# Storing dk of head 58 in pieces of 9, 112 and 7 rows, and dq and o in two parts each

## The chip, the cores and the metric

One core of one Trainium2 chip. Times are device microseconds (us) of a whole execution; lower is better. In the traces 16 DMA engines serve the core.

## The reference, cut to what matters

```python
def _fwd_reference(q, k, v):                       # q: 2 x 32 x 1 x 128, k and v: 2 x 32 x 8192 x 128, bf16
    scale = q.shape[-1] ** -0.5
    scores = jnp.einsum("bhqd,bhkd->bhqk", q, k) * scale
    p = _softmax(scores, axis=-1)
    return jnp.einsum("bhqk,bhkd->bhqd", p, v)

def reference(q, k, v, grad_out):                  # [cut: wrapping]
    _out, _vjp = jax.vjp(_f, q, k, v)
    return (_out, *_vjp(grad_out))                 # o, dq, dk, dv
```

There are 64 heads (2 x 32) with one query row each. k and v of a head are 2 MB each, and dk and dv are as large. So the work is 128 loads and 128 stores of 2 MB, 537 MB in all, around little arithmetic.

## The kernel before

A tile holds k or v of one head: 128 rows (partitions) of 64 x 128 values, 16384 bytes a row. Twelve such tiles circulate. dk and dv are written into the same tile that k and v came in; it can be loaded again only when its store has landed.

```python
    def by_rows(eng, dst, src, rows):
        p = 0
        for m in rows:                             # one DMA for each piece of m rows
            pin(eng.dma_start(out=dst[p : p + m], in_=src[p : p + m], max_dma_last_dim=NT * D))
            p += m
```

The stores go out from GpSimd's queue (`store_eng`, q0 in the profile), the loads from SyncE's (`load_eng`, q1). dv and dk of the last head, in four pieces each, go out from SyncE too. Eight heads have dk split into 126 + 2 rows; all the others, head 58 among them, go as one DMA of 128 rows:

```python
SPREAD = range(4, 60, 7)                           # heads 4, 11, ... 53
# [cut]
            if w == 0 and i in SPREAD:
                by_rows(store_eng, dst, h.tile[w], (P - 2, 2))
            else:
                eng = load_eng if len(ends) > 1 else store_eng
                pin(eng.dma_start(out=dst[:, b0:b1, :], in_=h.tile[w][:, b0:b1, :]))
```

At the very start six rows of q are loaded from GpSimd after its engine cursor has been reset (`FIRST = 6`), which by the rule that the prediction quotes below leaves the cursor at 6. At the end dq and o, 64 rows of 256 bytes each, go out in one DMA each:

```python
    for w, (src, dst) in enumerate(((dqT, out_1), (oT, out_0))):
        # [cut: transpose on TensorE and copy into nat]
        load_eng.dma_start(out=dst.rearrange("b h s d -> (b h s) d"), in_=nat[:BH, 0, :])
```

## Time and profile before

| | before |
|---|---|
| median of the first three runs | 1282.16 us (1280.69 to 1282.3) |
| span of the profiled run, clock | 1284.2 us, 0.941 |
| data moved | 539 MB, 420 GB/s on average |
| last compute | about 1262 us |
| last landing | 1282.8 us |

The lines that say what bounds this kernel stand in the prediction below. The timeline of GpSimd before, from 1160 us on; its columns are start, length, engine, line, operation, what is written from what, and in brackets the idle time ahead of it and what ended that:

```profile
1167.96 0.53 POOL L445 DMA_DIRECT2D out_dram<-kvt  x1 [14.62 <-DVE kvt L427]
1176.11 0.53 POOL L445 DMA_DIRECT2D out_dram<-kvt  x1 [7.62 <-DVE qb L187]
1186.32 0.53 POOL L445 DMA_DIRECT2D out_dram<-kvt  x1 [9.68 <-DVE kvt L427]
1194.47 0.53 POOL L445 DMA_DIRECT2D out_dram<-kvt  x1 [7.63 <-DVE qb L187]
1205.72 0.53 POOL L445 DMA_DIRECT2D out_dram<-kvt  x1 [10.72 <-DVE kvt L427]
1213.88 0.53 POOL L445 DMA_DIRECT2D out_dram<-kvt  x1 [7.62 <-DVE qb L187]
```

The first line is dk of head 58, the next five are dv and dk of 59, dv and dk of 60, and dv of 61. Each is issued once VectorE has made its values (`DVE`). None waits for an earlier store here.

### The profile page before, as it was taken

Reading aid. Unit: us, or ns where it says so; the run is one execution under the profiler, and the core shown is the slowest. Engines: PE = TensorE matmul, PEld = TensorE weight load, DVE = VectorE, ACT = ScalarE, POOL = GpSimd, SP = SyncE. Lnnn points to the kernel's source line nnn. Section 1 sums busy time; section 2 is a strip of 40 time slices with the busy share of each in tenths; the row PEclk is TensorE's granted clock in tenths of the full one; section 3 lists DMA queues with packets and bytes.
Section 4 is the critical chain, followed back from the end, with each engine's and each line's share of the span. In section 5 each row is a group of like instructions: output and inputs, shape, how many; then the busy total and the mean of one; then the engine's idle time right before and its main releaser. Section 6 shows DMA issues by size and latency. Waiting matters only on the chain.

```text
span 1284.2 us, 32475 instructions
## 1 busy us (share of the span) xinstructions
PE 1099.4 (86%) x14148; PEld 805.5 (63%) x14148; DVE 1014.6 (79%) x2258; ACT 956.9 (75%) x641; POOL 76.0 (6%) x143
## 2 busy tenths in 40 slices
PE   6899899899889899889899889888888799879870
PEld 5666666666666666666666666666656566656650
DVE  2888888888888888888888888888788688777882
ACT  6777777778778778778778778777778687777750
POOL 0000000000000000000000000000000000000000
PEclk9999999999999999999999999999999899999985
DMA  9999999999999999999999999999999999999995
GB/s 388 427 428 428 428 429 428 427 428 428 428 428 428 420 428 428 428 424 426 428 428 418 425 428 428 422 418 426 428 427 419 422 429 429 426 423 429 428 413 219
DMA packets 40155, 539.03 MB, mean 420 GB/s; under 512 B 5196, under 2 KB 5196, under 8 KB 6476
## 3 DMA queue, kind: packets, MB, share of 16 engines
q1 hardware_dynamic: 20172, 272.70, 49.9%
q0 software_dynamic: 19840, 264.25, 48.8%
q8 instruction: 110, 1.80, 0.5%
q14 instruction: 33, 0.27, 0.1%
HBM read 268.47 MB, written 268.47 MB: 418 GB/s over the span
## 4 chain that ended last, share of the span: by engine, by line
DVE 32%; DMA 17%; issue 14%; another core or an unknown queue 14%; PE 12%; ACT 8%; POOL 1%; SPq 0%; ACTq 0%; POOLq 0%; DVEq 0%
DVE kvt L427 18%; DMA kvt<-in_v_dram 11%; ACT ev L196 8%; PE tp L194 7%; DMA out_dram<-kvt 6%; DVE sel L395 4%; DVE rows L221 3%; DVE sel L389 1%; PE acc L372 1%; DVE pair L303 1%; PE raw L208 1%; ACT E_f L271 1%; DVE dSu L349 1%; PE sw L178 1%
## 5 line engine op out<-in xcount | busy, mean ns | idle before, releaser
L196 ACT COPY ev<-tp 128x2048 bf16<-128x2048 bf16 x512 | 941.3, 1868 | 285.7 <-PE tp L194 280.6
L427 DVE TENSOR_TENSOR kvt<-qb,pair 128x2048 bf16<-128x2048 bf16 x512 | 616.9, 1216 | 0.1
L194 PEld LDWEIGHTS <-kvt 128*128 128x128 bf16 x8192 | 507.0, 102 | 160.7 <-issue 114.4
L194 PE MATMUL tp<-ident_bf,kvt 128*128 128x128 bf16 x8192 | 572.9, 226 | 38.0 <-DMA kvt<-in_v_dram 28.8
L208 PE MATMUL raw<-ev,qdT 128*32 128x512 bf16 x2048 | 210.0, 399 | 5.0 <-ACT ev L196 1.6
L395 DVE SCALAR_TENSOR_TENSOR sel<-acc,diag,sel 128x128 f32<-128x128 f32 x384 | 134.7, 351 | 13.6
L228 PEld LDWEIGHTS sw<-sel,rows 128*128 128x128 f32 x1024 | 124.8, 192 | 29.7 <-issue 12.9
L228 PE MATMUL sw<-sel,rows 128*128 128x16 f32 x1024 | 137.2, 266 | 0.6 <-DVE rl L324 0.6
L372 PE MATMUL acc<-kvt,E_pad 128*32 128x512 bf16 x1024 | 102.9, 391 | 30.6 <-DVE E_pad L280 30.6
L445 POOL DMA_DIRECT2D out_dram<-kvt x118 | 63.3, 536 | 1081.9 <-DVE kvt L427 518.1
L372 PE MATMUL acc<-kvt,dS_pad 128*32 128x512 bf16 x1024 | 111.1, 426 | 0.8 <-DVE dS_pad L358 0.8
L221 DVE COPY rows<-raw 128x512 f32<-128x512 f32 x128 | 87.5, 684 | 26.1 <-PE raw L208 26.1
L178 PE MATMUL sw<-ident_bf,qdT 128*128 128x128 bf16 x128 | 28.5, 223 | 70.9 <-DVE mp L240 70.8
L280 DVE CAST E_pad<-E_f 128x64 bf16<-128x64 f32 x64 | 12.5, 195 | 92.9 <-ACT E_f L271 92.9
L208 PEld LDWEIGHTS <-qdT 128*32 128x32 bf16 x2048 | 64.6, 95 | 25.0 <-issue 18.4
L315 PEld LDWEIGHTS sw<-ld,ones 128*128 128x128 f32 x256 | 38.2, 188 | 54.5 <-issue 29.3
L372 PEld LDWEIGHTS <-E_pad 128*32 128x32 bf16 x1024 | 26.3, 93 | 55.2 <-DVE E_pad L280 40.1
L246 DVE TENSOR_REDUCE gm<-sw 1x1 f32<-1x128 f32 x64 | 17.9, 279 | 49.3 <-PE sw L244 49.3
L409 PE MATMUL acc<-ones,sel 128*128 128x1 f32 x256 | 47.5, 255 | 6.2 <-DVE sel L395 6.2
L315 PE MATMUL sw<-ld,ones 128*128 128x1 f32 x256 | 49.1, 261 | 0.1
L409 PEld LDWEIGHTS acc<-ones,sel 128*128 128x128 f32 x256 | 44.0, 215 | 7.3 <-DVE sel L395 7.3
L389 DVE TENSOR_SCALAR sel<-acc,diag 128x128 f32<-128x128 f32 x128 | 43.8, 342 | 0.0
(49 smaller groups left out, 367.5 us busy)
## 6 DMA issues: line engine op xcount, KB each, us to landing
out_dram<-kvt POOLq DMA_DIRECT2D x118, 2048.0 KB, 51.5
kvt<-in_v_dram SPq DMA_DIRECT2D x64, 2048.0 KB, 19.1
kvt<-in_k_dram SPq DMA_DIRECT2D x63, 2048.0 KB, 19.4
out_dram<-kvt POOLq DMA_DIRECT2D x8, 2016.0 KB, 55.7
out_dram<-kvt SPq DMA_DIRECT2D x8, 512.0 KB, 23.2
kvt<-in_k_dram SPq DMA_DIRECT2D x2, 512.0 KB, 4.5
kvt<-in_k_dram SPq DMA_DIRECT2D x1, 1024.0 KB, 7.2
out_dram<-kvt POOLq DMA_DIRECT2D x8, 32.0 KB, 55.2
```

The lines of the kernel that those rows point to most:

```text
L194: pin(nc.tensor.transpose(tp[:, t, :], src[:, c * CH + t, :], ident_bf[:]))
L196: pin(nc.scalar.copy(out=ev[:], in_=tp[:]))
L208: nc.tensor.matmul(h.raw[g * SW : (g + 1) * SW, :], lhsT=qdT[:, w, q0 : q0 + SW], rhs=ev[:, g * QT : (g + 1) * QT, :].rearrange("p n d -> ...
L221: pin(nc.vector.tensor_copy(out=h.rows[:], in_=h.raw[:]))
L228: nc.tensor.matmul(h.score[w].rearrange("p (n t) -> p n t", t=QT)[:, :, t], lhsT=h.rows[:, t * P : (t + 1) * P], rhs=sel4[:].rearrange("p ...
L315: nc.tensor.matmul(out, lhsT=ones[:].to_broadcast([P, P]), rhs=col, start=True, stop=True)
L372: nc.tensor.matmul(h.acc[w][g : g + CW, :], lhsT=wts[:, n0 : n0 + CW], rhs=rows[:, n0 : n0 + QT, :].rearrange("p n d -> p (n d)"), start=( ...
L389: nc.vector.tensor_scalar(out=h.sel[:], in0=block, scalar1=diag[:, 0:1], scalar2=None, op0=ALU.mult)
L395: nc.vector.scalar_tensor_tensor(out=h.sel[:], in0=block, scalar=diag[:, b : b + 1], in1=h.sel[:], op0=ALU.mult, op1=ALU.add,)
L409: nc.tensor.matmul(h.acc[w][:, 0:1], lhsT=h.sel[:], rhs=ones[:], start=True, stop=True)
L427: nc.vector.tensor_tensor(out=h.tile[w][:, n0 : n0 + CH, :].rearrange("p n (e t) -> p n e t", t=2), in0=h.qb[w][:] .rearrange("p (e t) -> ...
L445: pin(eng.dma_start(out=dst[:, b0:b1, :], in_=h.tile[w][:, b0:b1, :]))
```

## The change

The intent, from its title: dk of head 58 is stored as 9, 112 and 7 rows so that two DMA engines (13 and 14) carry fewer rows near the end, and dq and o go out in two parts each. The title's "sums in four column groups" has no line in the diff; both kernels have that.

```diff
+LATE = 58
...
-            if w == 0 and i in SPREAD:
+            if w == 0 and i == LATE:
+                by_rows(store_eng, dst, h.tile[w], (9, P - 16, 7))
+            elif w == 0 and i in SPREAD:
                 by_rows(store_eng, dst, h.tile[w], (P - 2, 2))
...
-        load_eng.dma_start(out=dst.rearrange("b h s d -> (b h s) d"), in_=nat[:BH, 0, :])
+        rows = dst.rearrange("b h s d -> (b h s) d")
+        p = 0
+        for m in (44, 20) if w == 0 else (42, 22):
+            load_eng.dma_start(out=rows[p : p + m], in_=nat[p : p + m, 0, :], max_dma_last_dim=D)
+            p += m
```

## The prediction

> **What bounds the kernel now**
>
> I read the page from the top: the slices and queue totals first, then the queue's own waits, then the stretches, then the transfers of the last 20 us alone.
>
> ```profile
> PE 1099.4 (86%) x14148; PEld 805.5 (63%) x14148; DVE 1014.6 (79%) x2258; ACT 956.9 (75%) x641; POOL 76.0 (6%) x143
> ...
> DMA  9999999999999999999999999999999999999995
> GB/s 388 427 428 428 428 429 428 427 428 428 428 428 428 420 428 428 428 424 426 428 428 418 425 428 428 422 418 426 428 427 419 422 429 429 426 423 429 428 413 219
> ...
> q1 hardware_dynamic: 20172, 272.70, 49.9%
> q0 software_dynamic: 19840, 264.25, 48.8%
> ```
>
> No compute engine is full. The 16 DMA engines are, in every slice but the last: loads (q1) and stores (q0) take 98.7% of them at 428 GB/s. The time is data over DMA rate, plus two ends.
>
> ```profile
> SPq L100 <- DMA out_dram<-kvt: 1138.7, 116, 25.0
> ```
>
> The load queue spends 1138.7 us waiting for earlier stores to land: a tile is loaded again once its store is complete on all 16 engines, so the slowest engine paces the rest.
>
> ```profile
> 1180.00:1245.00 65.00, 53.53 (x725) 38.77 (x722) 51.85 (x114) 48.93 (x34) 3.19 (x7) 1.00 0.99 422
> 1245.00:1262.00 17.00, 7.89 (x42) 4.54 (x42) 15.49 (x35) 0.00 (x0) 0.53 (x1) 0.51 0.97 408
> 1262.00:1284.00 22.00, 0.00 (x0) 0.00 (x0) 0.01 (x1) 0.00 (x0) 0.00 (x0) 0.50 0.33 136
> ```
>
> Stretches: length, busy time of PE, weight loads, DVE, ACT, POOL, then clock, DMA share, GB/s. Compute ends at 1262; the last 22 us are DMA alone, one third busy. Which third, the same stretch in slices of 0.5 us from 1264 shows:
>
> ```profile
> GB/s 328 205 322 256 180 266 195 213 238 180 221 221 213 180 238 190 194 165 119 115 78 25 66 57 12 33 25 25 25 25 25 33 25 25 25 25 4 0 0 16
> ```
>
> One engine moves 16384 B in 0.6075 us (from one packet's start to the next's in the packet records), 27 GB/s. So half the engines are done by 1268, and the row of 25s, 1276.5 to 1282.1, is ONE engine finishing alone. The 16 landings of the last transfer (o) say it per engine: eight by 1267.9; six at 1272.7 to 1274.7; one at 1276.70; one at 1282.79, after which only 1.4 us of closing waits come. That one engine lags in all late stores: dk of head 58 lands there at 1233.6, on the next at 1222.7. Its landings come 9.72 us apart, 16 rows of 0.6075: it never idles. The end is therefore that engine's total of work, and a row taken off it is 0.61 us.
>
> **What the Trainium skill says**
>
> "DMA: Bandwidth & Descriptors", section "Why a DMA increments its semaphore by 16 and not by 1": a transfer runs on the largest k up to 16 that divides its rows; from GpSimd, on k consecutive engines from a cursor. The trace agrees for the 126 + 2 stores: stringing packets together (each starts 3 to 4 ns before the end of the one before on its engine) gives 14 engines with 18 packets of 8192 B and two with 2. For 112 rows the rule says k = 16, seven rows each, and nothing would be uneven. The change's title says otherwise; see the first rival.
>
> Same page, "Queues, rings and completion order": each engine takes turns between its queues, packet by packet. The trace agrees: the 9.72 us hold 8 store rows and 8 load rows.
>
> Same page, "Latency and other measured facts": engines 7 and 15 are usually slower. The records have no engine numbers, but one strung chain has 1251 packets some 30 ns too long. It is one of the two that the 126 + 2 splits relieve, and is not late at the end. The laggard is another engine: it has full-speed packets, plus the instruction packets of 16 KB (110 in all, about 0.95 us each) that only eight chains carry, 13 or 14 each.
>
> **The change part by part**
>
> 1. dk of head 58. Before, eight packets of 16384 B on every engine: 8 x 0.6075 = 4.86 us. After, in packets of 8192 B (0.3055 us). Nine rows leave the cursor nine further on. If the 112 run on 14 engines, eight rows each, and seven rows follow, then with the cursor at 6 (set by the six q rows, unmoved by a pair 14 + 2) the pieces cover 6 to 14; 15 to 12; 13 to 3. Engines 13 and 14 get one row from the first and one from the last: two rows, exactly the title. They need 4 x 0.3055 = 1.22 us, about 0.1 us more for the 4-byte packets that a left-out engine got in the earlier splits, so they save 3.5 us. The engines with nine rows pay 18 x 0.3055 - 4.86 = +0.64 us.
>
> 2. dq and o. 64 rows on 16 engines, four each, become 44 + 20 and 42 + 22: by the rule 11, 10, 14 and 11 engines, the lowest ones. Rows of 256 B take 0.014 us: an engine that loses all eight saves 0.11 us. Two more issues on SP at 0.5 us, hidden behind 20 us of DMA.
>
> 3. Side effect on POOL. The order of instructions shows each store waiting for the one eight issues before it; two more issues shorten that reach. The 7-row piece waits for dk of 55 (landed 1174.4, ready at 1168). dv of 59 waits for dv of 56 (1184.2 instead of 1176.1), then dk 59 1193.9 for 1186.3, dv 60 1203.6 for 1194.5, dk 60 1213.4 for 1205.7, dv 61 1224.5 for 1213.9: 8 to 11 us late. No load waits for these stores (the last load, issued at 1213.5, needs head 57), and the laggard has over 20 us of stores queued, so it never sees it. The five fast engines (dk 58 landed from 1183.5 on) lose some us and have 15 to spare. Cost on the path: 0.
>
> 4. Side effect on SP. The parts of o wait for the third and fourth piece of the last dv: landed 1270.3 and 1276.2 before. The fourth is the laggard's, so 1272.6 if it is relieved; with 1.5 us to the first landing (1265.6 to 1267.1 before), 1274. Hidden by 5 us.
>
> Sum: the laggard, if relieved, lands at 1282.79 - 3.5 - 0.1 = 1279.2. The next engine becomes 1276.70 + 0.64 = 1277.3 at worst, so the whole saving shows: -3.6 us, 0.28%. From the median: 1282.16 - 3.6 = 1278.6 us.
>
> **The rivals**
>
> A. The 112 rows run on 16 engines. Then every engine has 1 + 7 = 8 rows, the split does nothing and the end stays: 1282.1. For it: the rule as the page states it. Against: a title that names 13 and 14 fits only the 14-engine count, and the choice of 9 and 7 would be pointless.
>
> B. The relief misses the laggard. The trace does not number engines. For a hit: the laggard is one of the eight with instruction packets, as is one of the relieved 126 + 2 pair and not the other; if those eight are consecutive and that pair their upper edge, the pair nine further on is their lower edge, and the turn in which the instruction packets come makes the laggard the second from it. That is two guesses. On a miss the laggard takes nine rows: 1282.16 + 0.6 = 1282.8.
>
> C. The waits of parts 3 or 4 take the saving's place: a late o, or a fast engine that turns late. It would need 5 us more than worked out; then 1280 to 1282.
>
> D. A speed-up over 2% (25.6 us) would need the pace before 1168 to change; nothing earlier is touched. A slowdown of that size would need the POOL waits to stall loads, and none is left that depends on them.
>
> **Range and chances**
>
> The main line, 1278.6, gets somewhat over half; A and B share most of the rest at 1282.1 and 1282.8; C is small. Weighted, 1280.1; I move toward the main line: 1279.3. Timed runs of before span 1.6 us, so 1276.8 to 1283.2 holds all of these branches. Faster by over 2%: 0.005; within 2%: 0.99; slower: 0.005.
>
> **What would show each step right or wrong**
>
> Right: in the last transfer's landings the latest comes near 1279 instead of 1282.8, the row of 25s in the tail shrinks from 5.6 to about 2 us, and the six middle engines land some 0.6 us later. In the packet records 14 engines have 16 packets of 8192 B for the 112 rows; 14 packets on all 16 would mean rival A. A lone tail of six us or more with uneven packets means rival B. POOL's waits for stores near 1170 to 1225 should grow to 8 to 11 us each with no effect on the end; if SP's last wait is for dq or o by more than 1 us, it is rival C. Wrong altogether: a changed landing pace before 1168, or two engines sharing the end.

## The result, and the profile after

| | before | after |
|---|---|---|
| median (lowest to highest), 4 runs each | 1282.23 (1280.69 to 1283.23) | 1282.1 (1279.93 to 1285.8) |
| ratio, 95% interval | | 1.0003 (0.9978 to 1.0028) |
| span of the profiled run, clock | 1284.2, 0.941 | 1280.2, 0.935 |

A ratio here is the mean time of one kernel's runs over the mean of the other's in the same rounds, so it is not quite the ratio of the medians. The verdict is "same". The profiled runs alone would have told another story: 4.0 us less, close to the predicted 3.6.

**Those 4 us are not the change's.** Until dk of head 58 is stored the two programs are the same, so nothing before that can be an effect. The timeline of GpSimd around the split store of head 53 (`x2`), before:

```profile
1068.33 1.36 POOL L89 DMA_DIRECT2D out_dram<-kvt  x2 [11.10 <-DVE kvt L427]
```

and after:

```profile
1061.62 1.36 POOL L90 DMA_DIRECT2D out_dram<-kvt  x2 [9.55 <-DVE kvt L428]
```

The run of the changed kernel was ahead by 6.7 us 100 us before the change begins, and by 4.06 us (1167.96 against 1163.90) where it does begin. At the end, 115 us later, it is 4.0 us ahead. The stretch that the change can touch took as long as before.

**The rows were not moved.** The queue totals of the page after (packets, MB, share of the 16 engines):

```profile
q1 hardware_dynamic: 20314, 272.70, 50.0%
q0 software_dynamic: 20032, 264.25, 48.9%
```

q0 has 192 packets more than before (19840, in the prediction). Whole, dk of head 58 was 128 row packets and 16 of 4 bytes that report completion, 144 in all. In pieces, a row is two packets of 8192 B, 256 in all, and each of the three pieces has 16 reports, 48. That makes 304, so 32 more are left to explain. They are 4-byte packets for the engines that a piece leaves out, one for each packet of the others: seven engines are left out of the 9 rows (7 x 2 = 14) and nine out of the 7 rows (9 x 2 = 18). Together that is the 32, and it leaves none for the 112 rows: no engine was left out of them. On 14 engines of eight rows two would have been left out at 16 packets each, another 32. Stringing the packets of this run together engine by engine says the same: every one of the 16 engines has 16 packets of 8192 B for this head, eight rows, just as before.

**The tail.** GB/s after in slices of 0.5 us from 1260 us:

```profile
GB/s 362 295 221 372 238 216 262 249 164 229 229 170 259 238 147 238 197 164 238 205 197 205 233 154 207 164 163 131 71 50 51 25 25 25 25 33 6 0 0 0
```

The row of 25s, one engine alone, is about 2 us here against 5.6 us before. The prediction had named just this as a sign of success. But this same kernel, profiled once more (experiment 5; from 1264 us), has a row of 25s of about 6 us:

```profile
GB/s 328 256 215 246 205 191 225 233 188 205 238 180 238 221 172 229 213 205 183 127 53 51 16 25 25 33 33 27 25 25 33 25 25 25 6 0 0 16 0 0
```

and a kernel with dk of 58 whole can be without one (experiment 1), so the sign was worthless.

**GpSimd's waits**, the timeline after:

```profile
1163.90 1.26 POOL L90 DMA_DIRECT2D out_dram<-kvt  x2 [14.39 <-DVE kvt L428]
1171.81 0.56 POOL L90 DMA_DIRECT2D out_dram<-kvt  x1 [6.66 <-DMA out_dram<-kvt]
1181.82 0.57 POOL L448 DMA_DIRECT2D out_dram<-kvt  x1 [9.45 <-DMA out_dram<-kvt]
1191.53 0.55 POOL L448 DMA_DIRECT2D out_dram<-kvt  x1 [9.15 <-DVE kvt L428]
1201.23 0.53 POOL L448 DMA_DIRECT2D out_dram<-kvt  x1 [9.15 <-DMA out_dram<-kvt]
1210.95 0.53 POOL L448 DMA_DIRECT2D out_dram<-kvt  x1 [9.19 <-DVE rows L222]
1220.67 0.53 POOL L448 DMA_DIRECT2D out_dram<-kvt  x1 [9.19 <-DVE kvt L428]
```

The first line is the 9 and the 112 rows, the second the 7 rows, then dv and dk of 59, dv and dk of 60, dv of 61. The 7 rows waited 6.66 us for an earlier store to land (`<-DMA`), and from there each issue follows the one before by 9.7 us, the pace at which the slowest engine lands stores (9.72 us, in the prediction). Where the view names VectorE for such a wait (1191.53, 1210.95, 1220.67), the even pace suggests that the landing held it. Taking off this run's lead of 4.06 us, dv of 59 is 9.8 us later than before and dv of 61 10.9 us.

**SyncE's waits** that concern stores, after: line, what ended the wait, us in total, times, longest. L534 issues the parts of dq and o, L561 is the closing wait, L101 issues the loads.

```profile
SPq L101 <- DMA out_dram<-kvt: 1135.8, 116, 27.2
SPq L534 <- DMA out_dram<-kvt: 14.4, 3, 5.8
SPq L561 <- DMA out_dram<-kvt: 6.9, 4, 3.2
```

Before, the closing wait (L554) and the issue of dq and o (L528):

```profile
SPq L554 <- DMA out_dram<-kvt: 16.1, 5, 11.6
SPq L528 <- DMA out_dram<-kvt: 3.1, 1, 3.1
```

The extra parts wait longer (14.4 us for 3.1), but the closing wait shrinks (6.9 us for 16.1): the same wait for the last landings, taken in another place.

### The profile page after: what moved, and what is told of

Read it like the earlier page. It is cut to its first block, busy times and chain, and to the rows that moved or that the text cites. A ratio compares the mean times of both kernels' runs of the same rounds, so it can differ in the third digit from the quotient of the medians.

```text
span 1280.2 us, 32479 instructions
## 1 busy us (share of the span) xinstructions
PE 1106.6 (86%) x14148; PEld 809.8 (63%) x14148; DVE 1013.9 (79%) x2258; ACT 957.0 (75%) x641; POOL 77.3 (6%) x145
## 3 DMA queue, kind: packets, MB, share of 16 engines
q1 hardware_dynamic: 20314, 272.70, 50.0%
## 4 chain that ended last, share of the span: by engine, by line
DVE 44%; DMA 13%; PE 13%; issue 12%; ACT 11%; another core or an unknown queue 3%; POOL 1%; SPq 0%; ACTq 0%; POOLq 0%; DVEq 0%
DVE kvt L428 25%; ACT ev L197 10%; PE tp L195 8%; DMA out_dram<-kvt 7%; DMA kvt<-in_v_dram 6%; DVE sel L396 6%; DVE rows L222 4%; DVE sel L390 2%; DVE pair L304 2%; PE acc L373 1%; PE raw L209 1%; DVE dSu L350 1%; ACT E_f L272 1%; PE sw L179 1%
## 5 line engine op out<-in xcount | busy, mean ns | idle before, releaser
L396 DVE SCALAR_TENSOR_TENSOR sel<-acc,diag,sel 128x128 f32<-128x128 f32 x384 | 134.7, 351 | 13.6
```

The lines of the kernel that those rows point to most:

```text
L396: nc.vector.scalar_tensor_tensor(out=h.sel[:], in0=block, scalar=diag[:, b : b + 1], in1=h.sel[:], op0=ALU.mult, op1=ALU.add,)
```

## The experiments

Twelve runs in five groups; every kernel gave the right result. The kernel before ran beside them in each group: 11 runs, medians 1282.13, 1281.84, 1281.06 and 1280.94 us in groups 1 and 2 (one job), 3, 4 and 5, from 1278.2 to 1291.5 over all. The jobs ran on three chips (7, 1, 7 and 11 in this order), so times are compared within a job. One kernel's runs range over 1%, and effects of a few us are better read from a stretch of a trace than from a time.

Therefore I use numbers from each trace, worked out from its landing records. A is when dv of head 58, the last store issued before the disputed one, has landed on its slowest engine; the gap is how far that engine is behind the next one at A. B is from A to the last landing of all. The tail is how far the last engine is behind the next one in the last piece of the last dk, close to the end. A and the gap are the run's own history and no experiment but one (the two-head kernel) touches them; B and the tail are what the split can change. There is one profile of each kernel in a job, so B is compared across chips.

```
kernel (rows of dk 58)          A      gap     B     tail
before (128)                 1224.5   11.5   58.3    6.0
after (9,112,7)              1220.1    7.1   59.2    2.8
halves: dk alone (9,112,7)   1222.8   11.5   58.4    5.3
halves: dq, o alone (128)    1217.9    1.0   58.0    0.4
(2,126)                      1219.1    3.3   59.0    1.3
(9,98,14,7)                  1220.1    1.8   57.6    0.3
(9,119)                      1221.7    5.1   63.3    5.4
(119,9)                      1216.8    1.4   68.6    0.2
(5,54,69)                    1217.6    1.6   72.9   13.4
(28,34,9,57)                 1220.5    4.6   56.3    1.4
(12,65,51)                   1220.1    6.3   57.3    3.0
(28,34,9,57) again           1224.4   13.4   57.6    2.6
after again                  1223.0   12.3   59.2    6.2
```

The last landing of the profiled run after came 3.5 us earlier than before's. That is all in A (4.4 us less); B is 0.9 us more.

### 1. The two halves of the change

dk alone keeps the first part of the diff and stores dq and o whole:

```diff
+PARTS = {58: (9, 112, 7)}
-            if w == 0 and i in SPREAD:
+            if w == 0 and i in PARTS:
+                by_rows(store_eng, dst, h.tile[w], PARTS[i])
+            elif w == 0 and i in SPREAD:
```

> Only the split of dk of head 58 into 9, 112 and 7 rows; dq and o as before. Theory K16 (112 rows run on 16 engines, so every engine still stores 8 rows of this head): ratio 1.000 within the noise of about 0.25%, lone tail of the last engine as long as before (5 to 6 us after the last but one), 16384-byte and 8192-byte packet counts as in the changed kernel. Rival K14 (112 on 14 engines, two engines with two rows): two engines with 14 packets of 8192 B less; ratio 0.997 if one of them is the laggard, 1.0005 if not. Rival W (the shorter reach of POOL's completion counters costs time and hides a gain): POOL issues 8 to 11 us late after the split and the laggard's landings behind it further apart than 9.72 us.

Measured: median 1281.56 us (4 runs), ratio 0.9982 (0.9945 to 1.002), B 58.4.

dq and o alone has only the last hunk of the diff:

```diff
-        load_eng.dma_start(out=dst.rearrange("b h s d -> (b h s) d"), in_=nat[:BH, 0, :])
+        rows = dst.rearrange("b h s d -> (b h s) d")
+        p = 0
+        for m in (44, 20) if w == 0 else (42, 22):
+            load_eng.dma_start(out=rows[p : p + m], in_=nat[p : p + m, 0, :], max_dma_last_dim=D)
+            p += m
```

> Only the parts 44 + 20 and 42 + 22 of dq and o. All theories: ratio 1.000; at most 0.1 us of the laggard's 256-byte rows is gone. SP issues the last part of o late, when the fourth piece of the last dv has landed (about 1276 in a run like the one before), and it lands some 1.5 us after its issue on the engines that are done, still before the laggard's own last store. Rival: if it lands last, the end moves out by 1 us or more.

Measured: 1282.82 us (4 runs), ratio 0.9995 (0.9955 to 1.0034), B 58.0. Neither half does anything that can be resolved, so no gain of the one is eaten by the other. Its profile holds the more useful finding. GB/s in slices of 0.5 us from 1258 us:

```profile
GB/s 393 336 363 234 297 238 202 296 188 249 238 156 246 188 229 188 227 201 229 172 238 188 205 221 188 214 176 188 182 129 126 66 49 57 26 0 0 16 0 0
```

dk of 58 is whole here, as in before, and there is one slice of 26 where before had a row of 25s. So the lone engine at the end, on which the whole prediction was built, is not there in every run. It is the run's own history: in the five profiles in which every engine has eight rows of this head, in the order before, after, dk alone, after again, dq and o alone, the gap at A is 11.5, 7.1, 11.5, 12.3 and 1.0 us, and the tail 6.0, 2.8, 5.3, 6.2 and 0.4. What these profiles share is the coarser picture: half of the engines are late (in before eight land o by 1267.9 us, the other eight from 1272.7 on).

### 2. Pieces that do leave engines out

2 and 126 rows put 1 row on the engine at the cursor and its neighbour, and 9 on the others. 9, 98, 14 and 7 rows give what the title speaks of, since 98 does run on 14 engines: 3 rows on engines 13 and 14, 8 or 9 on the others. The edit is the value of `PARTS`:

```diff
-PARTS = {58: (9, 112, 7)}
+PARTS = {58: (2, 126)}
```

> dk of head 58 as 2 and 126 rows, the order of the earlier splits turned round: the two rows go to the two engines at the cursor (6 and 7 if counted from the first q rows), the 126 to the 14 others. Theory L6 (the laggard is the engine at the cursor, the first of the nine-row piece in the changed kernel, with one row more than the rest of its kind to go): the laggard stores 1 row instead of 8 and saves about 4.2 us; the next one, 6.1 us ahead of it, gets 9 rows and loses 0.6; the lone tail shrinks from 6.1 to 1 to 2 us; ratio 0.9967. Rival W or other laggard (the relief of an engine late in the run is eaten by later waits, or the laggard is another engine): the end stays, or 0.6 us later, ratio 1.000 to 1.0005, and the lone tail keeps 5 us or more.

```diff
-PARTS = {58: (9, 112, 7)}
+PARTS = {58: (9, 98, 14, 7)}
```

> dk of head 58 as 9, 98, 14 and 7 rows: 98 divides by 14 and not by 15 or 16, so it leaves out the two engines that the title of the change names (13 and 14 from the cursor); they store 3 rows, the engine at the cursor 9. Theory L6: the laggard gets 0.6 us more, lone tail 6 us or more, ratio 1.0005 (same within noise). Rival (13 and 14 are the late ones, and only the count of 112 went wrong): the lone tail shrinks by 3 us, ratio 0.9977.

Measured: 1280.99 us (6 runs), ratio 0.9995 (0.9962 to 1.0029), B 59.0 for 2 + 126; 1284.6 us (4 runs), ratio 1.0004 (0.9969 to 1.0039), B 57.6 for the other. The packets of q0 in the page of the second confirm the count of engines:

```profile
q0 software_dynamic: 20080, 264.25, 49.0%
```

That is 240 over before. Reckoned as above: 256 row packets and 64 reports, and for engines left out 14 (9 rows on nine), 28 (98 on 14: two engines, 14 packets each), 4 (14 on 14: two engines, 2 each) and 18 (7 on seven), less the 144 of the whole store: 240. So even the split that really takes five rows (3.0 us) off both engines 13 and 14 moves the time by nothing that shows, and B by less than 2 us. Relieving one or two engines leaves the others of the late half in their place. The short tails, 1.3 and 0.3 us, are what the hopeful theory of each text asked for, but B did not fall with them. In these two profiles the slowest engine was only 3.3 and 1.8 us behind the next at A, and the timed runs leave over 0.3% open. What relief is worth to an engine that is 11 us behind, as in the prediction's profile, they do not test.

### 3. More rows on chosen engines

If rows per engine decide the end, moving many must show. From the cursor at 6: 9 + 119 puts 17 rows on engines 15 and 0 to 5 and one on the others; 119 + 9 puts 17 on 6 to 12; 5 + 54 + 69 puts 24 on 6 and 23 on 4 and 5.

```diff
-PARTS = {58: (9, 112, 7)}
+PARTS = {58: (9, 119)}
```

> dk of head 58 as 9 and 119 rows. 119 = 7 x 17 runs on seven engines, so the nine engines at the cursor (6 to 14, among them the seven late ones with full rows and instruction packets) store 1 row of this head and the seven others 17. Theory R (the end is the latest engine's rows at 0.61 us each; rows on engines with slack are free): the seven late engines land 4.3 us earlier relative to their stores of head 57, the other seven 5.5 us later; the eight early ones finish some 10 us before the late ones in all profiles so far, so they use half of that, except the eighth late engine, if it is among them: it gets 5.5 us more and becomes the last. Ratio 0.997 where it is not the last, 0.999 where it is. Rival W (a late relief is given back by waits): landings at the late engines no earlier, ratio 1.000.

```diff
-PARTS = {58: (9, 112, 7)}
+PARTS = {58: (119, 9)}
```

> The same two pieces in the other order: 119 rows on the seven engines at the cursor (6 to 12, mostly late ones), 17 rows each, then 9 rows on the nine others, one each. Theory R: the late engines get 9 rows = 5.5 us more, all of it at the end: ratio 1.0043, lone or last engine 5.5 us after where it would be. Rival W or N (the end follows something else, the distribution of one head's rows does not matter beyond noise): ratio 1.000, and no difference from the run with nine first. Between the two orders theory R wants 0.5 to 0.7%.

```diff
-PARTS = {58: (9, 112, 7)}
+PARTS = {58: (5, 54, 69)}
```

> dk of head 58 as 5, 54 and 69 rows: 69 = 3 x 23 gives 23 rows each to three early engines (4, 5, 6 from the cursor), 1 row to 7 to 10 and 6 rows to the other nine. Theory R: four engines land 4.3 us earlier, nine 1.2 us earlier, the three early ones 9 us later and still not last, so the end is 1.2 us earlier where the last engine is one of the nine and up to 4.3 where it is one of the four: ratio 0.997 to 0.999. Rival N: 1.000. Theory F (the early engines have less slack than 9 us): the three become last, ratio above 1.000.

| rows | median (6 runs) | ratio, 95% interval | B |
|---|---|---|---|
| 9, 119 | 1284.73 | 1.0017 (0.9985 to 1.0049) | 63.3 |
| 119, 9 | 1292.96 | 1.0082 (1.0046 to 1.0118) | 68.6 |
| 5, 54, 69 | 1296.84 | 1.0132 (1.0086 to 1.0179) | 72.9 |

The second and third are slower, clear of the noise, and the tail of the third, GB/s from 1272 us in slices of 0.5 us, shows one overloaded engine for 13 us:

```profile
GB/s 147 147 98 127 74 33 57 66 28 41 41 0 41 8 33 41 8 33 33 41 0 49 8 33 41 8 33 41 8 33 33 8 33 25 25 12 0 0 0 16
```

So the rows do land where the rule puts them, and the end follows the late engines' rows. These three also told which engines are late. The packet chains, strung together, of the run after give for dv of 58, engine by engine: when it sent its report (the landing is recorded some 0.4 us later), and whether the chain has one of the 16-KB instruction packets (i) or an 8-KB one (j) within some 80 us:

```
early: 1170.8 i  1177.8   1178.7 (slow packets)  1179.6   1182.1   1187.6 j  1189.6   1191.3
late:  1206.5 j  1209.8 i 1211.2 i 1211.5 i 1211.6 i 1212.6 i 1212.7 i 1219.7 i
```

Seven of the eight engines with 16-KB instruction packets (110 in the execution, about 0.95 us each, in fixed turn) are late; the eighth is one of the two that the 126 + 2 splits relieve. From the number of 8192-B packets that each chain got in experiments 2 and 3 their places follow, counted from the cursor: 6, two of 8 to 10, 11 to 14, and one of 2 and 3. So the title's engines 13 and 14 are late ones, but two of eight. Which of them is the slowest at dv of 58 changes from run to run: it is one of 6 and 7 in the 2 + 126 run, and one of 13 and 14 in the 9, 98, 14, 7 run, so in both an engine that the split then relieves. In the first the packets show the relief at work: that engine lands dv of 59 at 1228.3 us, as the first of the late eight, and the last of them lands it at 1232.2.

Three of my expectations were off. For 9 + 119 I expected a ratio of 0.997 to 0.999 and measured 1.0017 (an interval that holds 0.999): the eighth late engine, one of 2 and 3, got nine rows more, and B grew by 5. I took the three engines of the 69 rows for early ones; the one at the cursor is late. And the cost is larger than the rows: nine rows more at 0.61 us are 5.5 us, B grew by 10; 16 rows are 9.8 us, B grew by 15. The packet records show stretched packets, enough for about the other 5 us. Summing, from 1165 us on, what store packets took beyond their usual length (611 ns for 16384 B, 309 ns for 8192 B; only those over by more than 60 ns) gives for all engines together 4.2 us before and 3.9 with dq and o alone, 13.6 after, 60 for 9 + 119, 42 for 119 + 9, 25 for 5 + 54 + 69. In the 119 + 9 run each of the seven engines with 17 rows has 2.9 to 6.1 us of it, the nine others 0.3 to 2.4. In the last run the engine that ended last has 6.4 us. Many rows on few engines is not the whole of it: splits that leave every engine eight rows have some too (14.2 in dk alone, 14.9 in after again), and 28, 34, 9, 57 of the next group has 30.7 and 23.0. What stretches the packets, no run shows. The loss also shows as rate. The stretch from 1180 to 1245 us (columns as in the prediction, the last is GB/s), after:

```profile
1180.00:1245.00 65.00, 56.35 (x715) 40.32 (x711) 55.24 (x126) 46.73 (x33) 4.30 (x8) 0.94 1.01 425
```

and with 9 + 119:

```profile
1180.00:1245.00 65.00, 54.20 (x705) 39.63 (x702) 49.94 (x111) 47.58 (x32) 3.22 (x6) 0.95 1.00 402
```

The DMA share is full in both, while 5% fewer bytes move.

### 4. Relieving all late engines together

If relief failed above because it never took in all eight, a split that takes in all should work. A search over pieces under the rule of the largest k gave 28, 34, 9, 57: on 14, 2, 9 and 3 engines, it leaves every late engine 2 or 3 rows, and puts 17 on engines 4 and 5 and 21 on 15, 0 and 1, all early. 12, 65, 51 is a milder one, and a third kernel does two heads.

```diff
-PARTS = {58: (9, 112, 7)}
+PARTS = {58: (28, 34, 9, 57)}
```

> dk of head 58 as 28, 34, 9 and 57 rows: by the rule of the largest count up to 16 that divides, on 14, 2, 9 and 3 engines. With the cursor at 6 every late engine (6, 9 to 14, and whichever of 2 and 3 is late) gets 2 or 3 rows instead of 8, engines 4 and 5 get 17 and engines 15, 0 and 1 get 21; those five are early ones. Theory (the end is the row total of the late engines, and relief showed nothing so far because it never took in all eight): five rows fewer on all of them, 5 x 0.61 = 3.0 us; the stretch from the slowest landing of dv 58 to the last landing, 57.6 to 59.2 us in the earlier profiles, becomes 55 to 56, and the time falls by 0.2 to 0.25%, at the edge of what five rounds resolve. Rival (the engines with 21 rows take their place): 13 rows more and some 5 us of stretched packets, 13 us against the 20 to 25 us by which they were ahead at dv 58; if that is not enough the stretch stays at 58 or over. Second rival (something other than the DMA rows holds the end): 58, with no lone tail.

```diff
-PARTS = {58: (9, 112, 7)}
+PARTS = {57: (28, 34, 9, 57), 58: (13, 64, 51)}
```

> As the run before it for head 57, then 13, 64 and 51 rows for head 58 (13, 16 and 3 engines, cursor from 2): late engines 2 or 3 and 5 rows instead of 8 and 8, so 8 to 9 rows less in all; engines 15, 0 and 1 get 21 and 22, 26 rows more in all. Theory: 8 x 0.61 = 4.9 us or 0.38% faster, if the three loaded engines, 16 us and the stretching later, still are not last. Rival (they become last): same or slower than before, with a lone tail of three engines in the last transfer. The split of head 57 also delays stores that loads still wait for; if that stalls loads, the waits of the load queue after 1160 grow and the time with them.

```diff
-PARTS = {58: (9, 112, 7)}
+PARTS = {58: (12, 65, 51)}
```

> dk of head 58 as 12, 65 and 51 rows (12, 13 and 3 engines): 5 or 6 rows on every late engine and on 4, 5, 7 and 8, and 18 on engines 15, 0 and 1. Theory: two rows fewer on all late engines, 1.2 us, too little for the timed runs to resolve; the stretch from the slowest landing of dv 58 to the end falls from 58.3 to about 57. Rival (the loaded engines become last): 58 or more.

| rows | median (6 runs) | ratio, 95% interval | B |
|---|---|---|---|
| 28, 34, 9, 57 | 1278.55 | 0.9972 (0.9952 to 0.9992) | 56.3 |
| two heads | 1290.68 | 1.0075 (1.0047 to 1.0103) | - |
| 12, 65, 51 | 1281.23 | 0.9993 (0.9969 to 1.0016) | 57.3 |

The first is the only kernel whose interval lies below 1. Its q0 packets:

```profile
q0 software_dynamic: 21008, 264.26, 49.2%
```

1168 more than before, of which 992 are 4-byte packets for engines left out of the four pieces (8, 476, 14 and 494): the rule's counts of 14, 2, 9 and 3 engines exactly. A left-out engine gets 72 of them from the 34 and the 57 rows, at 0.006 us some 0.4 us, so the relief of five rows is worth 2.6 us rather than 3.0; B fell by 2.0 (from 58.3).

With two heads the rival came true. Counted from the slowest landing of dv of head 57, the rest took 87.1 us against 79.2 before and 78.6 after. The last transfer's four latest landings are at 1279.5, 1280.3, 1284.5 and 1286.6 us, the other twelve by 1276.2, and the 51 rows of head 58 have landed on their slowest engines at 1230.2, 1231.2, 1235.2 and 1237.4, well after the 1221.1 of the twelfth: the loaded engines had become the last. (Four stand out where three are loaded. The packets tell them apart: the one that landed at 1231.2 got a run of 4-byte packets for the 51 rows, so it was left out; the other three moved 8192-B packets right up to their landing.) The early engines' lead is worth one such split, not two.

### 5. The best one again, beside the changed kernel

One interval below 1 among ten kernels can be chance, so it ran once more, with the changed kernel beside it; neither has an edit beyond those already shown.

> The kernel with 28, 34, 9 and 57 rows once more, unchanged, beside the changed kernel of the case and fresh runs of before. It was the one of ten kernels whose interval lay below 1 (0.9972), and one in ten can do that by chance at 95%. If the gain is real: ratio near 0.997 to 0.998 again, the slowest landing of dv 58 to the last landing again 55.5 to 57 us. If it was chance: ratio 0.999 to 1.002 and 58 or more.

> The changed kernel once more, for a direct comparison with the 28, 34, 9, 57 kernel on the same chip. Theory (112 rows run on 16 engines, so no engine's rows change): ratio 1.000 within 0.003, slowest landing of dv 58 to the last landing 58 to 59.5 us, 2 to 3 us more than the other kernel's.

Measured: 28, 34, 9, 57: 1280.59 us (6 runs), ratio 0.9993 (0.9972 to 1.0014), B 57.6. The changed kernel: 1283.02 us (6 runs), ratio 1.0018 (0.9993 to 1.0043), B 59.2. The gain of the first did not repeat at a size that can be resolved. Pooling both jobs, 12 runs with a mean of 1279.53 against 22 with 1281.52, is 0.9984, with an interval of about 0.0013 each way, but the first job was picked for being good, so that is flattering. B was expected at 55.5 to 57 if the gain was real and at 58 or more if not; 57.6 lies between. It keeps its order: 56.3 and 57.6 for this split, 58.0 to 59.2 in the five profiles in which every engine has eight rows (but 57.6, too, for 9, 98, 14, 7, which relieves only two). I take from this a relief of 1 to 2 us, about 0.1%, as possible; neither the times nor two profiles prove it. The changed kernel has by now ten timed runs with nothing gained.

## Why the prediction was right or wrong

**Right: the range.** 1282.1 us lies in 1276.8 to 1283.2. The point, 1279.3, is 2.8 us low. The range was drawn to hold the main line and every rival, so that it held says nothing for the mechanism; the main line, which got over half of the weight, failed at its first step.

**Wrong: the first term, "if the 112 run on 14 engines, eight rows each".** They ran on 16, seven rows each, so all engines kept eight rows and the saving of 3.5 us was 0. This is rival A in mechanism and number (1282.1). The page quoted in the prediction, "DMA: Bandwidth & Descriptors" of the Trainium skill, section "Why a DMA increments its semaphore by 16 and not by 1", gives k = 16 for 112 rows; the trace of before agreed with it for 126 rows; only the title's wording spoke against it, and I gave the title more than half. The weights were the mistake, not the sums.

**Wrong: "the end is therefore that engine's total of work", as if one engine always ended alone.** A lone engine did end four of the five profiles with eight rows on every engine (tails of 2.8 to 6.2 us), but not the one with dq and o alone (tail 0.4 us), and the slowest engine is not always the same one: one of 6 and 7 in one run, one of 13 and 14 in another. A fixed split of one or two engines can miss it, and the prediction's margin to "the next engine" was read from one profile. Whether a saving of 3.5 us on the right engine would show in a run with a gap of 11 us stays open: no run here relieved one or two engines in such a run. Its landings "9.72 us apart" are also not the whole story: they are for the stores up to dk of 57, while dv of 58 came 11.1 us and dk of 58 9.1 us after the one before.

**Wrong: rival B's picture of eight consecutive engines with instruction packets.** They are scattered (6, two of 8 to 10, 11 to 14, and the relieved one), and the late eighth has none of the 16-KB packets.

**Right: part 2,** dq and o in parts cost and gain nothing (ratio 0.9995). Their extra packets (q1 from 20172 to 20314) cost nothing that shows.

**Right: part 3,** the waits on GpSimd. With the run's lead of 4.06 us added back, dv of 59 went out at 1185.9 (predicted 1184.2), dk of 59 at 1195.6 (1193.9), dv of 60 at 1205.3 (1203.6), dk of 60 at 1215.0 (1213.4) and dv of 61 at 1224.7 (1224.5): right within 1.7 us, and free, as dk alone shows (B 58.4).

**Right: part 4,** o waits for dv's last piece: its second part went out at 1271.1 us, having waited for that piece's landing at 1271.07, and the end came at 1279.3 by the slow engines. The piece is the laggard's; it was the run's lead and not the relief that made it early.

**Misleading: the test I had set.** "The latest landing near 1279 instead of 1282.8" and "the row of 25s shrinks to about 2 us" both came true in the profiled run, with no row moved; profiled again, the same kernel had the latest landing at 1282.2 and a tail of 6.2 us. The test that held was the count of packets for the 112 rows; the prediction says 14 packets on all 16 engines would mean rival A, and that is what is there.

## What to carry to other kernels

Before a split by rows is timed, count the engines of each piece from the queue's packet totals: a piece that runs on all 16 moves nothing. When half the engines are late and the slowest changes from run to run, a split that relieves two of them gained nothing that could be measured. Rows piled on few late engines cost about twice what their number says (10 us for 5.5, 15 for 9.8), with stretched packets in the record. A tail that one profile shows is looked for in a second profile of the same kernel before a change is built on it. A difference of some us between two profiles is checked first at a point where both programs are still the same; here the whole of it was there already.

## What the Trainium skill lacked or had wrong

- "DMA: Bandwidth & Descriptors", section "Why a DMA increments its semaphore by 16 and not by 1": nothing wrong. The rule of the largest k up to 16 held for 112 (16), 98, 126 and 28 (14), 54 and 9 (9), 119 and 7 (7), 69, 57 and 51 (3) and 34 rows (2); the exception that it names for GpSimd (some copies on 16 engines whatever the rows) was not met. Lacking: engines left out of a GpSimd store get one 4-byte packet for each packet of the others. 28, 34, 9, 57 has 992 of them, at some 0.006 us each.
- The same page, section "Latency and other measured facts", expects engines 7 and 15 to be slow. One chain with packets some 30 ns too long is in each of the traces strung together but is early at the end here; it is one of the two that the 126 + 2 splits relieve. Seven of the eight late engines are those that carry 16-KB instruction packets, 110 of about 0.95 us each in fixed turn over eight engines. I found no page that says that these packets fall on only eight of the 16 engines. That they make those engines late, no run here tests.
- No page that I read says that packets of a store in pieces of rows are stretched: 4.2 us of it over all engines with dk of 58 whole, 13.6 to 14.9 us in three pieces with eight rows on every engine, 42 and 60 us with 17 rows on seven engines.
